# The first MLP product of eight of twelve chunks in Strassen's scheme: seven sub-products for eight, with overlaid buffers, a shared ring of PSUM banks and a new order of steps

## The chip, the cores and the metric

The kernel runs on one core of one Trainium2 chip. Times are device microseconds of that core for one execution. The kernel before takes 614.36 us (median of 3 runs, 613.46 to 614.62). Lower is better.

## The reference: what is computed

Attention over 4 batches of 8 heads, 768 positions and a head width of 64, in which a query sees its neighbours (distance under 16) and 24 block summaries. The result, laid out as 3072 rows of 512, goes through an MLP with a gelu between two products.

```python
k_sum = k.reshape(B, H, nb, block, D).max(axis=3)
v_sum = v.reshape(B, H, nb, block, D).mean(axis=3)
...
a = np.exp(scores_all)
a = a / (np.sum(a, axis=-1, keepdims=True) + 1e-09)
v_all = np.concatenate([v, v_sum], axis=2)
...
h = x @ w_in                                   # (3072, 512) @ (512, 2048)
g = 0.5 * h * (1.0 + erf(h * inv_sqrt2))
return (g @ w_out).astype(np.float32)          # (3072, 2048) @ (2048, 512)
```

## The kernel before

**Precision.** Every operand of a matmul is split into two float16 parts, hi (a cast) and lo (what the cast loses). A product is three matmuls: hi x hi, hi x lo and lo x hi. So each operand costs a cast (ScalarE, or GpSimd) and a subtraction (VectorE). The weights arrive as 64-bit floats; three bit operations on VectorE (`wi_bits`, `wo_bits`, lines 290, 295, 299) make float32 of them, `wi_hi` casts (line 306), and the lo part comes either from VectorE (line 321) or from two matmuls with an identity and a negative identity (`wi_diff`, lines 311 and 312) that ScalarE then reads (`wi_dlo`).

**Units and chunks.** The 3072 rows are 12 chunks of 256. Attention goes by 24 units: one chunk and four heads, two units to a chunk. A unit's steps: loads, `k_hi`, `q_hi`, `k_lo`, `q_lo`, `scores` (48 matmuls, line 558), `add_mask` (VectorE, line 569, reads PSUM), `maximum` over the partitions (GpSimd, line 578), `shift` (VectorE), `exponent` (ScalarE), `p_hi`, `p_lo`, `values` (52 matmuls, lines 623 and 632), a normalization of four VectorE steps (lines 643 to 657), and `x_hi`, `x_lo` (lines 671 and 675), the operand of the MLP.

**The MLP.** `phase1 c i` makes 256 of the 2048 hidden columns for chunk c: 24 matmuls of 256 columns (lines 694 to 696: two halves, four parts of the inner dimension, three products). Then `gelu` (ScalarE, line 701, from PSUM), `g_hi` (line 710) and `g_lo` (VectorE, line 714). `phase2 c i` is a quarter of the second product for half of the chunk's rows: 12 matmuls of 512 columns (lines 728 to 730), accumulated in PSUM; `store` and `put` bring the rows out. The last half chunk is cut in two columns (`phase2_cut`).

**Memory.** The eight PSUM banks are divided for good: two for the scores, two for the values, two for `phase1` (and the weight differences), two for `phase2`.

**Order.** Nothing is ordered by the compiler. `ORDER` is a list of steps written out by hand, 1315 of them; each step appends its instructions to the queues of the engines that it uses, and every engine works through its queue in that order. All DMAs are issued from one queue (SP), in the same order. A step that waits thus holds up all that stands behind it on its engine.

Of the kernel before, what the change touches and what calls it, by code (L numbers as in the profile page):

```python
# [58 lines left out]
k_lo 3, wi_hi 0, q_hi 2, p_lo 0, maximum 1, load_neg, f_mask 2, mean_vt, load_q 3, s_load_vs 0, q_lo 2, wi_diff 0 1,
fetch_w_in 6, v_hi 0, wi_diff 0 0, wi_dlo 0 1, wi_bits 1 0, scores 2, wi_dlo 0 0, wi_bits 1 1, v_diff 0 0,  # L60
s_load_vs 1, k_hi 4, fetch_w_in 5, shift 1, v_diff 0 1, v_hi 1, wi_bits 1 2, v_dlo 0 0, q_hi 3, exponent 1, warm 3,
v_diff 1 1, load_q 4, q_lo 3, v_dlo 0 1, load_v 2, p_hi 1, wi_bits 2 0, v_dlo 1 1, warm 2, values 0, wi_hi 1,
wi_bits 2 1, fetch_w_in 3, v_diff 1 0, norm_den 0, p_lo 1, evac 2, wi_diff 1 1, norm_take 0, v_dlo 1 0, f_mask 3,
maximum 2, load_mask, norm_rec 0, wi_dlo 1 1, norm_spread 0, load_k 6, scores 3, norm_mult 0, load_q 5, wi_diff 1 0,
evac 3, wi_bits 2 2, load_v 3, values 1, x_hi 0, k_hi 5, wi_dlo 1 0, x_lo 0, q_hi 4, wi_hi 2, shift 2, load_vs 2,
norm_den 1, warm 4, wi_diff 2 0, wi_bits 3 0, exponent 2, maximum 3, wi_diff 2 1, norm_take 1, load_k 7, v_hi 2,
norm_rec 1, norm_spread 1, wi_dlo 2 0, norm_mult 1, wi_dlo 2 1, warm 6, v_diff 2 0, wi_bits 3 1, x_hi 1, load_vs 3,
v_diff 2 1, v_dlo 2 0, x_lo 1, p_hi 2, v_hi 3, load_v 4, shift 3, phase1 0 0, v_dlo 2 1, q_hi 5, p_lo 2, exponent 3,
phase1 0 1, wi_bits 6 0, gelu 0 0, p_hi 3, wi_bits 6 1, load_vs 4, g_hi 0 0, p_lo 3, phase1 0 2, gelu 0 1, g_hi 0 1,
wi_bits 3 2, wi_bits 6 2, wi_hi 3, values 2, gelu 0 2, g_lo 0 0, fetch_w_in 4, wi_diff 3 0, wi_hi 6, k_lo 5,  # L70
wi_diff 3 1, g_lo 0 1, wi_dlo 3 0, g_hi 0 2, k_lo 4, wi_diff 6 0, wi_dlo 3 1, wi_bits 5 0, wi_dlo 6 0, wi_diff 6 1,
wi_bits 5 1, v_hi 4, phase1 0 3, wi_bits 5 2, wi_dlo 6 1, norm_den 2, wi_bits 4 0, fetch_w_in 7, wi_hi 5, norm_take 2,
v_diff 3 0, gelu 0 3, norm_rec 2, wi_bits 4 1, g_hi 0 3, wi_diff 5 1, v_dlo 3 0, g_lo 0 3, wi_dlo 5 1, wi_diff 5 0,
wi_bits 4 2, v_diff 3 1, wi_dlo 5 0, norm_spread 2, wi_hi 4, fetch_w_out 0, phase1 0 5, load_v 5, norm_mult 2,
v_dlo 3 1, wi_bits 7 0, x_hi 2, wi_bits 7 1, wi_diff 4 1, gelu 0 5, wi_bits 7 2, g_hi 0 5, wi_diff 4 0, wi_dlo 4 1,
g_lo 0 5, fetch_w_out 4, wi_hi 7, values 3, x_lo 2, wi_dlo 4 0, wo_bits 0 0, phase1 0 6, norm_den 3, wi_lo 7,
load_vs 5, norm_take 3, v_hi 5, norm_rec 3, phase1 0 7, norm_spread 3, gelu 0 6, norm_mult 3, g_hi 0 6, wo_bits 4 0,
x_hi 3, wo_bits 4 1, phase1 0 4, gelu 0 7, g_hi 0 7, x_lo 3, g_lo 0 6, g_lo 0 2, phase1 1 1, wo_bits 0 1, gelu 0 4,
# [5 lines left out]
fetch_w_out 6, wo_bits 5 1, wo_bits 5 2, phase2 0 1, wo_lo 3, wo_hi 5, fetch_w_out 7, q_lo 4, phase2 0 3, wo_lo 5,
load_q 6, q_lo 5, wo_bits 6 0, phase2 0 5, wo_bits 6 1, wo_bits 6 2, load_q 7, phase2 0 2, wo_bits 7 0, wo_hi 6,
fetch_k 1 0, wo_bits 7 1, wo_bits 7 2, scores 4, phase2 0 4, wo_lo 6, q_hi 6, wo_hi 7, fetch_v 1 0, k_hi 6,
add_mask 4, wo_lo 7, scores 5, maximum 4, add_mask 5, phase2 0 6, k_lo 6, g_lo 1 0, q_hi 7, load_k 8, phase2 0 7,
store 0 0, shift 4, k_hi 7, put 0 0, g_lo 1 2, exponent 4, maximum 5, v_lo 4, phase2 1 1, gelu 1 4, p_hi 4, q_lo 6,
phase2 1 3, load_v 6, store 0 1, shift 5, load_q 8, g_hi 1 4, put 0 1, p_lo 4, exponent 5, phase2 1 0, q_lo 7,
g_lo 1 4, p_hi 5, load_q 9, g_lo 1 5, phase2 1 2, prep_v 1 0, values 4, p_lo 5, phase2 1 4, norm_den 4, g_lo 1 7,  # L90
norm_take 4, gelu 1 6, norm_rec 4, norm_spread 4, phase2 1 5, norm_mult 4, g_hi 1 6, v_lo 5, x_hi 4, g_lo 1 6,
load_v 7, values 5, x_lo 4, prep_k 1 0, phase2 1 7, norm_den 5, norm_take 5, fetch_k 1 1, fetch_v 1 1, prep_k_end 1 0,
norm_rec 5, k_sums 1 0, phase2 1 6, norm_spread 5, store 1 1, norm_mult 5, put 1 1, k_lo 7, x_hi 5, x_lo 5, load_k 9,
scores 6, phase1 2 0, add_mask 6, q_hi 8, k_hi 8, prep_k 1 1, maximum 6, phase1 2 2, gelu 2 0, prep_k_end 1 1,
fetch_k 2 0, g_hi 2 0, store 1 0, prep_v 1 1, put 1 0, k_sums 1 1, phase1 2 1, gelu 2 2, g_hi 2 2, shift 6,
fetch_k 3 1, load_vs 7, phase1 2 7, gelu 2 1, g_lo 2 2, g_hi 2 1, g_lo 2 0, exponent 6, load_vs 6, q_lo 8, phase1 2 6,
k_lo 8, load_q 10, g_lo 2 1, gelu 2 7, p_hi 6, load_k 10, prep_k 3 1, scores 7, gelu 2 6, p_lo 6, v_hi 6, phase1 2 4,
q_hi 9, k_hi 9, g_hi 2 6, add_mask 7, g_hi 2 7, v_lo 6, v_hi 7, maximum 7, phase1 2 3, gelu 2 4, v_lo 7, load_v 8,
g_hi 2 4, values 6, gelu 2 3, g_hi 2 3, shift 7, phase2 2 1, norm_den 6, norm_take 6, exponent 7, load_v 9, g_lo 2 7,
load_vs 8, g_lo 2 3, phase2 2 0, k_lo 9, p_hi 7, norm_rec 6, load_k 11, norm_spread 6, p_lo 7, phase2 2 3, load_vs 9,  # L100
v_hi 8, norm_mult 6, v_lo 8, x_hi 6, values 7, x_lo 6, load_v 10, q_lo 9, phase2 2 2, norm_den 7, g_lo 2 6, load_q 11,
v_hi 9, norm_take 7, norm_rec 7, v_lo 9, scores 8, load_vs 10, norm_spread 7, phase1 2 5, q_hi 10, norm_mult 7,
k_hi 10, add_mask 8, x_hi 7, load_v 11, x_lo 7, maximum 8, scores 9, gelu 2 5, q_lo 10, phase1 3 0, g_hi 2 5,
load_vs 11, g_lo 2 5, q_hi 11, phase1 3 3, shift 8, gelu 3 0, k_hi 11, g_hi 3 0, load_q 12, g_lo 3 0, exponent 8,
q_lo 11, phase1 3 2, k_lo 10, add_mask 9, load_k 12, gelu 3 3, p_hi 8, load_q 13, g_lo 2 4, scores 10, maximum 9,
g_hi 3 3, p_lo 8, phase1 3 7, gelu 3 2, g_hi 3 2, q_hi 12, g_lo 3 2, phase1 3 5, gelu 3 7, k_hi 12, g_hi 3 7, shift 9,
g_lo 3 7, exponent 9, phase1 3 4, g_lo 3 3, k_lo 12, add_mask 10, gelu 3 5, p_hi 9, values 8, q_lo 12, maximum 10,
phase2 2 5, norm_den 8, p_lo 9, load_q 14, gelu 3 4, v_hi 10, g_hi 3 5, phase1 3 6, v_lo 10, g_hi 3 4, g_lo 3 4,
load_v 12, g_lo 3 5, phase1 3 1, gelu 3 6, norm_take 8, g_hi 3 6, shift 10, g_lo 3 6, phase2 2 7, exponent 10,
norm_rec 8, norm_spread 8, norm_mult 8, k_lo 11, gelu 3 1, p_hi 10, values 9, prep_k 2 0, load_k 13, scores 11,  # L110
g_hi 3 1, prep_k_end 2 0, v_hi 11, phase2 2 4, fetch_v 2 0, q_hi 13, g_lo 3 1, fetch_k 3 0, k_sums 2 0, q_lo 13,
x_hi 8, k_hi 13, load_k 14, v_lo 11, store 2 1, phase2 2 6, load_q 15, k_lo 13, put 2 1, load_v 13, x_lo 8,
# [749 lines left out]
```

## Time and profile before

| | |
|---|---|
| median of 3 runs | 614.36 us |
| profiled execution: span from its first to its last instruction | 612.4 us |
| TensorE (PE) busy | 604.4 us, 6050 matmuls |
| VectorE (DVE) busy | 396.4 us, 442 instructions |
| ScalarE (ACT) busy | 291.3 us, 413 instructions |
| GpSimd (POOL) busy | 162.0 us, 107 instructions |
| TensorE's granted clock | 0.999 on average |

The profile records one execution. A row of the groups gives line, engine, operation, output and inputs, count, busy time, mean nanoseconds of one, and the engine's idle time before them with what ended it. A row of the timeline gives start and duration in us. Matmuls are pipelined: the recorded duration of one (0.27 us for 256 columns) is longer than the distance to the next. The profiled execution's time beside its span is not recorded apart; its span lies 2.0 us under the median of the runs.

### The profile page before, as it was taken

The page shows a single profiled execution, that of the slowest core. Times are in us where ns is not written, and L with a number is a line of the kernel's source. Part 1 is how long each engine was busy: PE and PEld are TensorE (multiplying, and loading weights), DVE is VectorE, ACT ScalarE, POOL GpSimd, SP SyncE. Part 2 cuts the span into 40 slices and gives each one's busy share as a digit, 9 for nine tenths or more (in the row PEclk, how much of TensorE's full clock was granted, in tenths as well). Part 3 has the DMA queues.
Part 4 walks back from the last instruction along what each step waited for, and adds up shares of the span by engine and source line. Part 5 has one row for each costly group of instructions (what it writes and reads, how often), then busy time and mean ns, then how long its engine had stood idle before and what let it go on. Part 6 is the DMA issues. An engine that isn't in the chain of part 4 may idle for free.

```text
span 612.4 us, 13632 instructions
## 1 busy us (share of the span) xinstructions
PE 604.4 (99%) x6050; PEld 400.1 (65%) x6050; DVE 396.4 (65%) x442; ACT 291.3 (48%) x413; POOL 162.0 (26%) x107
## 2 busy tenths in 40 slices
...
GB/s 337 389 233 70 253 158 191 226 124 174 178 127 135 83 224 192 87 136 36 47 74 56 28 192 17 6 105 30 3 59 76 1 3 18 1 35 1 1 34 35
DMA packets 27306, 63.92 MB, mean 104 GB/s; under 512 B 2480, under 2 KB 6576, under 8 KB 26672
## 3 DMA queue, kind: packets, MB, share of 16 engines
...
HBM read 54.99 MB, written 6.29 MB: 100 GB/s over the span
## 4 chain that ended last, share of the span: by engine, by line
PE 85%; DVE 9%; DMA 2%; issue 2%; POOL 1%; ACT 1%; DVEq 0%; POOLq 0%
PE pso L728 13%; PE pso L729 13%; PE pso L730 13%; PE psh L694 12%; PE psh L695 12%; PE psh L696 12%; PE pss L558 3%; PE psv L632 2%; PE psv L623 2%; DMA kp<-in_kp_dram 1%; POOL m L578 1%; DVE wst_i L295 1%; DVE pl L594 1%; DVE ks L397 1%; PE psw_i L311 1%
## 5 line engine op out<-in xcount | busy, mean ns | idle before, releaser
L694 PE MATMUL psh<-xh,w_in_h 128*128 128x256 f16 x768 | 209.5, 273 | 0.4 <-ACT g L701 0.3
L695 PE MATMUL psh<-xl,w_in_h 128*128 128x256 f16 x768 | 209.3, 273 | 0.5 <-DVE xl L675 0.5
L696 PE MATMUL psh<-xh,w_in_l 128*128 128x256 f16 x768 | 209.3, 273 | 0.0
L728 PE MATMUL pso<-w_out_h,gh 128*128 128x512 f16 x368 | 139.7, 380 | 0.0
L729 PE MATMUL pso<-w_out_l,gh 128*128 128x512 f16 x368 | 139.5, 379 | 0.0
L730 PE MATMUL pso<-w_out_h,gl 128*128 128x512 f16 x368 | 139.5, 379 | 0.0
L714 DVE SCALAR_TENSOR_TENSOR gl<-g,gh 128x512 f16<-128x512 f32 x96 | 71.3, 758 | 90.0 <-ACT gh L710 89.8
L701 ACT ACTIVATE g<-psh 128x512 f32<-128x512 f32 x96 | 56.9, 595 | 116.3 <-PE psh L696 116.0
L578 POOL PARTITION_ALL_REDUCE m<-s x24 | 85.1, 3546 | 49.8 <-DVE s L569 37.3
L694 PEld LDWEIGHTS <-w_in_h 128*128 128x128 f16 x768 | 75.1, 98 | 12.0 <-issue 1.0
L695 PEld LDWEIGHTS <-w_in_h 128*128 128x128 f16 x768 | 75.2, 98 | 11.4 <-issue 0.9
L696 PEld LDWEIGHTS <-w_in_l 128*128 128x128 f16 x768 | 75.1, 98 | 9.3 <-issue 0.7
L710 ACT ACTIVATE gh<-g 128x512 f16<-128x512 f32 x96 | 58.9, 627 | 20.6 <-PE pso L729 18.5
L730 PEld LDWEIGHTS <-gl 128*128 128x128 f16 x368 | 36.0, 98 | 43.4
L728 PEld LDWEIGHTS <-gh 128*128 128x128 f16 x368 | 36.0, 98 | 40.2
L729 PEld LDWEIGHTS <-gh 128*128 128x128 f16 x368 | 36.1, 98 | 39.2
L590 POOL CAST ph<-s 128x1024 f16<-128x1024 f32 x24 | 31.0, 1291 | 93.1 <-PE psv L632 50.6
L532 POOL CAST qh<-q 128x512 f16<-128x512 f32 x22 | 19.8, 900 | 135.3 <-PE pss L558 135.3
L600 DVE SCALAR_TENSOR_TENSOR v_lo<-v,v_hi 128x1024 f16<-128x1024 f32 x20 | 29.3, 1470 | 22.8 <-ACT v_hi L597 22.8
L594 DVE TENSOR_TENSOR pl<-s,ph 128x1024 f16<-128x1024 f32 x24 | 34.7, 1444 | 13.0 <-POOL ph L590 13.0
L583 DVE TENSOR_TENSOR s<-s,m 128x1024 f32<-128x1024 f32 x24 | 34.7, 1444 | 11.4 <-POOL m L578 11.2
L735 ACT ACTIVATE ot<-pso 128x512 f32<-128x512 f32 x23 | 13.6, 593 | 47.6 <-PE pso L730 42.3
...
## 6 DMA issues: line engine op xcount, KB each, us to landing
...
```

The costliest lines, as they stand in the source:

```text
L578: nc.gpsimd.partition_all_reduce(out_ap=self.m32, in_ap=self.s32, channels=P, reduce_op=bass_isa.ReduceOp.max)
L583: nc.vector.tensor_tensor(out=self.s32, in0=self.s32, in1=self.m32, op=ALU.subtract)
L594: nc.vector.tensor_tensor(out=self.pl, in0=self.s32, in1=self.ph, op=ALU.subtract)
L694: nc.tensor.matmul(ph[:, e, :], w_in_h[:, k, fs], xh[:, k, :], start=(k == 0), stop=False)
L695: nc.tensor.matmul(ph[:, e, :], w_in_h[:, k, fs], xl[:, k, :], start=False, stop=False)
L696: nc.tensor.matmul(ph[:, e, :], w_in_l[:, k, fs], xh[:, k, :], start=False, stop=(k == NCC - 1))
L701: nc.scalar.activation(g32, pht.pop((c, i)), AF.Gelu, scale=1.0 / (SC_X * SC_WI))
L710: nc.scalar.activation(gh, g32t[c, i], AF.Copy, scale=SC_G)
L714: nc.vector.scalar_tensor_tensor(out=gl, in0=g32t.pop((c, i)), scalar=SC_G, in1=gh, op0=ALU.mult, op1=ALU.subtract)
L728: nc.tensor.matmul(p, gh[:, f, js], w_out_h[:, f, :], start=(f == 0), stop=False)
L729: nc.tensor.matmul(p, gh[:, f, js], w_out_l[:, f, :], start=False, stop=False)
L730: nc.tensor.matmul(p, gl[:, f, js], w_out_h[:, f, :], start=False, stop=(f == NFC - 1))
```

## The change

The chunks 4 to 11 are taken by pairs (4 and 5, 6 and 7, and so on). For a pair, x is a matrix of two by two blocks: A11 and A12 the even chunk's two halves of the inner dimension, A21 and A22 the odd chunk's; `w_in` has B11, B12, B21, B22 by halves of the inner dimension and of the hidden columns. Four blocks of the result take eight block products as they stand. Strassen's scheme, in Winograd's form, takes seven:

- S1 = A21 + A22, S2 = S1 - A11, S3 = A11 - A21, S4 = A12 - S2 (`sx_add`, on VectorE, for every pair); T1 = B12 - B11, T2 = B22 - T1, T3 = B22 - B12, T4 = B21 - T2 (`t_add`, once);
- P1 = A11 B11, P2 = A12 B21, P3 = S4 B22, P4 = A22 T4, P5 = S1 T1, P6 = S2 T2, P7 = S3 T3, each a `product` of 12 matmuls for a column group j (256 columns of each half; j from 0 to 3);
- the results are P1 + P2 (even chunk, first half), P1 + P6 + P5 + P3 (even, second), P1 + P6 + P7 + P4 (odd, first) and P1 + P6 + P7 + P5 (odd, second).

P1, P6, P7 and P4 are accumulated one after the other in one PSUM bank; between them `keep` (ScalarE) copies the state to SBUF three times, and `h_add` (VectorE) adds a copy to another bank, for three of the four results. `gelu` then works in place. The sums S and T get hi and lo parts of their own: seven x casts and subtractions for a pair instead of four, and eight `t_hi` and `t_lo`.

The float32 words of `w_in` are kept (`w32`) until the T are made, and the parts of T are written over them. To make room, tiles share memory: the staging tile later holds x parts and sums, `k32` first holds `w_out` words, the identity lies in the mask's tile and the output tile in the 16-bit mask's, hsum lies over the part of `w_in` that only chunks 0 to 3 use, and `p_h`, `p_l` and the x parts have one copy or fixed places. The scores and the values keep two PSUM banks each; all else takes the next free bank of a ring of four. In batch 0 and around, many casts go from GpSimd to ScalarE (`s_k_hi` 14 times for 2, `s_q_hi` 12 for 2, `s_p_hi` 16 for 0, `s_load_vs` 5 for 2). The order, now 1536 steps, is written anew from the first step to the last.

```diff
+PAIRS = (2, 3, 4, 5)
+class Ring:
+    def use(self, key, uses):
+        if key not in self.held:
+            self.held[key] = [self.free.pop(0), 0]
+        tenant = self.held[key]
+        tenant[1] += 1
+        if tenant[1] == uses:
+            self.free.append(self.held.pop(key)[0])
+        return tenant[0]
...
-fetch_k 0 0, load_m16, load_q 0, fetch_k 0 1, fetch_vt 0, prep_k 0 0, s_k_hi 0, load_ind, warm 20, f_mask 0,
+load_q 0, fetch_k 0 0, k_hi 0, s_q_hi 0, q_lo 0, prep_k 0 0, k_lo 0, prep_k_end 0 0, k_sums 0 0, fetch_w_in 0,
...
+load_v 1, fetch_w_in 1, evac 0, s_k_hi 1, load_neg, wi_hi 0 0, wi_hi 0 1, warm 1 4, f_mask 1, wi_diff 0 0, wi_dlo 0 0,
+prep_k_end 0 1, wi_diff 0 1, k_sums 0 1, k_lo 1, warm 2 1, scores 1, s_k_hi 2, s_q_hi 2, maximum 0, shift 0, q_lo 2,
+wi_bits 2 0, k_lo 2, wi_dlo 0 1, evac 1, exponent 0, maximum 1, s_p_hi 0, s_k_hi 3, sum_vt 0, sum_vt 1, sum_vt 2,
+mean_vt, f_mask 2, scores 2, shift 1, p_lo 0, wi_bits 2 1, wi_bits 1 0, wi_bits 2 2, wi_bits 1 1, k_lo 3, wi_bits 1 2,
...
+sx_lo 2 1, norm_mult 10, t_lo 0 0, p_lo 11, shift 12, k_lo 13, phase2 3 3, phase2 3 6, values 11, product 2 0 1,
+product 2 0 2, phase2 3 5, t_lo 0 1, norm_den 11, load_v 12, norm_take 11, norm_rec 11, norm_spread 11, norm_mult 11,
...
+product 2 0 7, sx_add 2 6, p_sx_hi 2 6, keep 2 0 2, t_add 3 2, h_add 2 1 0, t_add 2 3, sx_lo 2 6, k_lo 14,
...
+    ps_s = ps.tile([P, UCOLS], F32, name="ps_s")
+    ps_v = ps.tile([P, UCOLS], F32, name="ps_v")
+    bank = Ring("bank", [ps.tile([P, 512], F32, name=f"bank{i}") for i in range(4)])
...
+    hsum = [late[:, i * 1024 : (i + 1) * 1024].bitcast(F32) for i in range(3)]
+    w32 = [const.tile([P, 2, WP], F32, name=f"w32_{i}") for i in range(4)]
...
+    wst_ring = Ring("wst", [k32[:, :WP]])
...
+    def t_add(i, n):
+        b11, b21, b12, b22 = (w32[i][:, f, k * 512 : (k + 1) * 512] for f in range(2) for k in range(2))
+        out, in0, in1, op = (
+            (b22, b22, b12, ALU.subtract), (b12, b12, b11, ALU.subtract),
+            (b11, b22, b11, ALU.add), (b21, b21, b11, ALU.subtract),
+        )[n]
+        nc.vector.tensor_tensor(out=out, in0=in0, in1=in1, op=op)
+    def t_hi(i, e):
+        dst = t_hl[i][0].rearrange("p t k f -> p (t k f)")[:, e * WP : (e + 1) * WP]
+        nc.scalar.activation(dst, w32[i][:, e], AF.Copy, scale=SC_WI)
+    def t_lo(i, e):
+        h, l = (a.rearrange("p t k f -> p (t k f)")[:, e * WP : (e + 1) * WP] for a in t_hl[i])
+        nc.vector.scalar_tensor_tensor(out=l, in0=w32[i][:, e], scalar=SC_WI, in1=h, op0=ALU.mult, op1=ALU.subtract)
...
+    PRODUCTS = {
+        1: (SX, A11, (0, 0), True), 6: (SX, S2, T2, False), 7: (SX, S3, T3, False), 4: (SX, A22, T4, False),
+        2: (SY, A12, (1, 0), True), 5: (SZ, S1, T1, True), 3: (SZ, S4, (1, 1), False),
+    }
+    USES = {SX: 8, SY: 2, SZ: 4}
+    def acc(p, j, a):
+        return bank.use(f"s{p}_{j}{a}", USES[a])
+    def product(p, j, m):
+        a, xi, w, first = PRODUCTS[m]
+        t = acc(p, j, a)
+        xh, xl = x_hl[xi]
+        for e in range(2):
+            dst = t[:, e * CH : (e + 1) * CH]
+            for k in range(KH):
...
+                for n, (l, r) in enumerate(((wh, xh), (wh, xl), (wl, xh))):
+                    nc.tensor.matmul(
+                        dst, l, r[:, k], start=(first and e == 0 and k == 0 and n == 0),
+                        stop=(k == KH - 1 and n == 2), skip_group_check=True,
+                    )
+    def keep(p, j, n):
+        nc.scalar.activation(hsum[n], acc(p, j, SX), AF.Copy)
+    def h_add(p, j, n):
+        c, i = 2 * p + n // 2, j + 4 * (n % 2)
+        g = g_ring.use(f"{c}_{i}", 4)
+        a, s = ((SY, 0), (SZ, 1), None, (SZ, 2))[n]
+        nc.vector.tensor_tensor(out=g, in0=acc(p, j, a), in1=hsum[s], op=ALU.add)
...
-    nc = _bacc.Bacc("TRN2", target_bir_lowering=False, num_devices=1)
+    nc = _bacc.Bacc("TRN2", target_bir_lowering=False, num_devices=1, dynamic_dma_scratch_size=512)
```

More of the change, by code (lines that the diff above doesn't have):

```diff
@@ L59 @@
[L59 to L78, printed above, removed]
@@ L84 @@
[L84 to L103, printed above, removed]
@@ L104 @@
[L104 to L112, printed above, removed]
-prep_v 2 0, phase2 3 1, norm_den 9, prep_k 3 0, fetch_k 2 1, phase2 3 3, load_k 15, add_mask 11, fetch_v 2 1,
@@ new lines @@
+phase2 1 7, add_mask 6, norm_take 5, norm_rec 5, norm_spread 5, norm_mult 5, load_k 8, fetch_v 3 0, s_q_hi 8,
+s_k_hi 8, maximum 6, q_lo 8, load_vs 6, put 0 1, x_hi 5, store 1 0, x_lo 5, q_lo 7, shift 6, phase1 2 2, phase1 2 0,
+v_hi 6, t_add 1 0, t_add 2 0, v_lo 6, k_lo 8, put 1 0, load_vs 7, load_k 9, fetch_k 2 0, load_q 10, load_k 10,
+exponent 6, v_hi 7, store 1 1, v_lo 7, load_v 9, load_q 9, scores 7, phase1 2 1, add_mask 7, scores 8, s_p_hi 6,
+q_hi 10, s_k_hi 9, p_lo 6, values 6, phase1 2 4, prep_k 2 0, add_mask 8, gelu 2 0, k_lo 9, gelu 2 2, gelu 2 1,
@@ new lines @@
+norm_rec 7, norm_spread 7, g_lo 2 4, prep_k_end 2 1, g_lo 2 5, norm_mult 7, g_hi 2 6, x_hi 7, scores 9, load_k 12,
+put 1 1, load_q 12, fetch_v 2 0, t_add 1 1, x_lo 7, add_mask 9, prep_v 3 0, t_add 3 0, load_k 11, phase1 3 6,
+phase1 3 2, exponent 8, g_hi 2 7, s_p_hi 8, maximum 9, k_hi 11, g_lo 2 6, prep_v 2 0, scores 10, gelu 3 6, p_lo 8,
+add_mask 10, shift 9, gelu 3 2, phase1 3 0, phase1 3 5, values 8, fetch_v 3 1, load_q 11, load_v 10, fetch_k 3 1,
+prep_v 3 1, g_lo 2 7, k_lo 11, t_add 1 2, prep_k 3 1, gelu 3 5, norm_den 8, norm_take 8, norm_rec 8, gelu 3 0,
@@ new lines @@
+prep_v 2 1, q_lo 12, g_lo 3 3, norm_den 9, norm_take 9, shift 11, phase2 2 5, phase2 3 0, phase2 2 7, t_add 2 1,
+g_hi 3 4, v_hi 11, t_add 2 2, prep_k_end 3 0, store 2 0, norm_rec 9, g_lo 3 4, sx_hi 2 0, v_hi 10, norm_spread 9,
+sx_lo 2 0, v_lo 11, exponent 11, g_lo 3 5, t_hi 0 1, g_hi 3 7, g_lo 3 7, p_lo 10, phase2 3 2, scores 12, phase2 3 4,
+v_lo 10, t_add 0 3, norm_mult 9, values 10, p_sx_hi 2 1, norm_den 10, add_mask 12, put 2 0, store 2 1, t_hi 0 0,
+norm_take 10, norm_rec 10, norm_spread 10, phase2 3 1, load_k 13, s_k_hi 13, s_p_hi 11, k_hi 14, maximum 12,
@@ new lines @@
+load_k 17, k_hi 17, add_mask 15, load_vs 15, load_q 17, maximum 15, s_q_hi 17, k_lo 16, load_k 18, p_hi 14, gelu 5 6,
+h_add 2 3 1, gelu 4 7, p_sx_hi 3 0, g_hi 5 6, v_hi 15, norm_den 13, g_hi 4 7, product 2 3 4, phase2 4 5, phase2 5 1,
+g_lo 5 2, k_lo 17, shift 15, v_lo 14, g_lo 4 7, phase2 4 6, scores 16, p_lo 14, sx_lo 3 0, norm_take 13, phase2 4 7,
+norm_rec 13, norm_spread 13, g_hi 5 7, q_lo 17, v_lo 15, norm_mult 13, values 14, add_mask 16, load_v 16, put 3 1,
+k_sums 3 0, gelu 5 3, store 4 0, norm_den 14, g_hi 5 3, exponent 15, prep_k_end 3 1, norm_take 14, norm_rec 14,
```

651 lines of the change are left out of this document (368 added, 283 removed).

## The prediction

> **What bounds the kernel now.** The page of the profile comes first: its span and its busy times.
>
> ```profile
> span 612.4 us, 13632 instructions
> PE 604.4 (99%) x6050; PEld 400.1 (65%) x6050; DVE 396.4 (65%) x442; ACT 291.3 (48%) x413; POOL 162.0 (26%) x107
> ```
>
> TensorE is busy 99% of the span, but a busy share does not say whether the work is needed or dense. So I read the span in three stages, cut where the first product begins (46.26) and where chunk 4 begins (236.33).
>
> ```profile
> core 0: us, PE busy (x) PEld busy (x) DVE busy (x) ACT busy (x) POOL busy (x), PEclk, DMA share, GB/s
> 0.00:46.26 46.26, 43.18 (x413) 19.20 (x414) 40.22 (x40) 29.40 (x41) 29.73 (x26) 1.00 0.85 317
> 46.26:236.33 190.07, 188.22 (x1986) 126.83 (x1986) 179.17 (x189) 110.33 (x150) 61.29 (x38) 1.00 0.52 164
> 236.33:612.40 376.07, 373.04 (x3658) 254.03 (x3652) 176.99 (x214) 151.55 (x222) 70.96 (x44) 1.00 0.16 48
> ```
>
> The clock is at 1.00 throughout. In the last stage VectorE (DVE) works 177 of 376 us: TensorE alone sets the time. In the middle one DVE works 179 of 190: it is nearly as late as TensorE. Then the density, in order of time (start, duration):
>
> ```profile
> 480.32 0.27 PE L694 MATMUL psh<-xh,w_in_h 128*128 128x256 f16 x1
> ...
> 482.94 0.27 PE L694 MATMUL psh<-xh,w_in_h 128*128 128x256 f16 x1
> ```
>
> ```profile
> 536.30 0.38 PE L728 MATMUL pso<-w_out_h,gh 128*128 128x512 f16 x1
> ...
> 538.89 0.38 PE L728 MATMUL pso<-w_out_h,gh 128*128 128x512 f16 x1
> ```
>
> Between the first pair of rows lie 24 matmuls (one `phase1`): 2.62/24 = 0.109 us each, back to back. Between the second lie 12 (one `phase2`): 2.59 us. A matmul taken out of this stream is worth its 0.109.
>
> **The change part by part. Removed.** For each pair of chunks and each of four column groups j, eight sub-products of 12 matmuls become seven: 16 x 12 = 192 matmuls fewer, of the same 256 columns. 192 x 0.109 = **20.9 us** off TensorE. Start-up matmuls (`warm`) fall from 52 to 40, but these fill waits and give nothing by themselves.
>
> **Start-up.** What ends last before the first product is DVE's `x_lo 1`:
>
> ```profile
> 5.37 1.75 DVE L397 TENSOR_REDUCE ks<-w_out_l 128x48 f32<-128x1536 f32 x1 [5.37 <-DMA w_out_l<-in_kp_first_dram]
> ...
> 10.57 0.81 DVE L539 TENSOR_TENSOR k_lo<-w_out_l,k_hi 128x640 f16<-128x640 f32 x1
> ```
>
> ```profile
> 12.16 2.51 DVE L539 TENSOR_TENSOR k_lo<-w_out_l,k_hi 128x640 f16<-128x640 f32 x1
> ```
>
> ```profile
> 12.05 3.27 POOL L578 PARTITION_ALL_REDUCE m<-s  x1
> ```
>
> ```profile
> 46.10 1.52 DVE L675 TENSOR_TENSOR xl<-den,xh 128x512 f16<-128x512 f32 x1
> ```
>
> ```profile
> 73.18 0.69 DVE L714 SCALAR_TENSOR_TENSOR gl<-g,gh 128x512 f16<-128x512 f32 x1 [0.43 <-ACT gh L710]
> 73.79 0.68 DVE L675 TENSOR_TENSOR xl<-den,xh 128x512 f16<-128x512 f32 x1
> ```
>
> The same `k_lo` takes 0.81 us alone and 2.51 beside a GpSimd maximum (+1.69, rounded apart); `x_lo` takes 0.68 alone and 1.52 beside a GpSimd cast. From the 2.51 row to the 46.10 row, and one cast just before, 13 DVE instructions are stretched so, 9.7 us in all. With 5.4 us of waiting for the first load that leaves 47.6 - 15.1 = 32.5 us of DVE work up to the end of `x_lo 1`. The new order asks for three more bit steps (two of L290, one of L299):
>
> ```profile
> 60.58 0.70 DVE L290 TENSOR_SCALAR wst_i<-wraw_i 128x1024 int32<-128x1024 int32 x1
> 61.31 1.23 DVE L295 SCALAR_TENSOR_TENSOR wst_i<-wraw_i,wst_i 128x1024 int32<-128x1024 int32 x1
> 62.57 1.23 DVE L299 SCALAR_TENSOR_TENSOR wst_i<-wraw_i,wst_i 128x1024 int32<-128x1024 int32 x1
> ```
>
> 2 x 0.73 + 1.2 = 2.7, so 35.2. GpSimd loses most of its casts to ScalarE (ACT) here: six instructions, three of them maxima, instead of sixteen with four. I take a little over half of the stretch: 5.2. The first load now stands behind `load_q 0`: 6 instead of 5.4. A new wait: `shift 1` stands on DVE only 2.1 us of work behind `shift 0`, while `maximum 1` must first see two `wi_diff`, `scores 1`, `evac 1`; I estimate 3 us (0 to 4; 3.3 is one whole maximum), and all DVE work behind it is late by that. `x_lo 1` then ends at 35.2 + 6 + 5.2 + 3 = 49.4, and the first product starts, as now, 1.4 before: 48. Ahead of it stand two more `wi_diff` and two more `v_diff`, each
>
> ```profile
> 61.08 1.02 PE L311 MATMUL psw_i<-wst_i,eye 128*128 128x512 f32 x2
> 61.94 0.38 PE L312 MATMUL psw_i<-w_in_h,neg 128*128 128x512 f16 x1
> 62.15 0.27 PE L694 MATMUL psh<-xh,w_in_h 128*128 128x256 f16 x1
> ```
>
> 1.07 us, which later stages need no more: 46.26 + 4.3 = 50.5 would be no change, so start-up gains **2.5**. Bounds: a gain of 8 (neither stretch nor wait) and a loss of 5 (ACT, busy 29.4 us now and given the casts, some 8 us, becomes the late one).
>
> **Middle stage,** first product to the first Strassen product. It gains two `phase2`, one `values` and one `scores`:
>
> ```profile
> 117.19 0.81 PE pss L558 x48
> ...
> 137.15 0.55 PE psv L623 x4
> 137.70 0.76 PE psv L632 x48
> ```
>
> 5.2 + 1.3 + 0.8 less the 4.3 moved out: 190.07 + 3.0 = 193.1 if TensorE sets it. DVE gets 13 of the 16 `t_add`, three more `prep_v`, and a unit's steps earlier. Prices: `t_add`, `sx_add`, `sx_lo` and `h_add` by L675 above, whose neighbour starts 0.6 apart; the rest from
>
> ```profile
> L600 DVE SCALAR_TENSOR_TENSOR v_lo<-v,v_hi 128x1024 f16<-128x1024 f32 x20 | 29.3, 1470 | 22.8 <-ACT v_hi L597 22.8
> L735 ACT ACTIVATE ot<-pso 128x512 f32<-128x512 f32 x23 | 13.6, 593 | 47.6 <-PE pso L730 42.3 <-DMA out_dram<-ot 5.2
> ```
>
> ```profile
> L450 DVE TENSOR_REDUCE vs<-vb 96x64 f32<-96x2048 f32 x6 | 13.6, 2275 | 1.3 <-DMA vb<-in_vb_dram 1.3
> ```
>
> (`prep_v` 2.3 by L450; `t_lo` by L600's form, 1.47 at most as its mean holds stretched ones, and nearer the 1.23 of L299). DVE's 179.2 holds 17.8 of stretch, in 20 instructions from the 46.10 row to
>
> ```profile
> 220.16 1.17 DVE L545 TENSOR_TENSOR ql<-q,qh 128x512 f16<-128x512 f32 x1 [0.93 <-POOL qh L532]
> ```
>
> so 161.4 net. Added are 7.8 (`t_add`) and 6.9 (`prep_v`), and 5 for the rest: `add_mask`, two `shift`, `p_lo`, a normalization (2.4, below), two `prep_k_end`, two `sx_lo`, a `t_lo` are 10, and two `x_lo`, a `q_lo` and three bit steps go, 5. Together 181. What stretch comes on top? A normalization beside a maximum is not stretched:
>
> ```profile
> 34.82 0.70 DVE L643 STREAM_TRANSPOSE dent<-den 128x512 f32<-128x512 f32 x1
> ...
> 36.67 0.69 DVE L657 TENSOR_TENSOR den<-psv,dent 128x512 f32<-128x512 f32 x1
> ```
>
> ```profile
> 34.22 3.77 POOL L578 PARTITION_ALL_REDUCE m<-s  x1 [2.86 <-ACT s L565]
> ```
>
> In the new order a reduction or a normalization step stands first or second after `add_mask` 4 to 12, where the maximum starts (all but 8); the old order has a `v_lo`, `p_lo` or `q_lo` in that place, 1.69 longer, for six of these nine. I take 4 us of stretch (0 to 17.8): DVE needs 185 of 193. All `kp` and `vb` loads now come in this stage, since their tile holds x later; L450's row shows 1.3 us of waiting for them, and I add none. DVE begins about 1 us late, so I charge **+1.5** (0 to +10: 181 + 17.8 = 199, some waits, against 193.1).
>
> **Last stage.** TensorE needs what it needs now less 20.9 and the steps moved forward (7.3). New beside it: 48 `keep` on ACT (L735's form, 0.593: 28.5 us), 48 `h_add` (28.8), 16 `sx_add`, 12 more `sx_lo`, the last `t_lo` on DVE: at most 177.0 + 28.8 + 9.6 + 7.2 + 8.5 + 1.8 = 233 us, while ACT has 151.6 + 28.5 + 8.5 (`t_hi`) + 7.6 (`sx_hi`) + 9 (casts) = 205, both in 348: covered. What can show is the handover. Products 1, 6, 7, 4 share one bank; each must wait until `keep` has copied the state before. The latency:
>
> ```profile
> 609.15 0.22 PE L746 MATMUL pso<-w_out_h,gl 128*128 128x128 f16 x1
> ```
>
> ```profile
> 609.41 0.28 ACT L749 ACTIVATE ot<-pso 128x128 f32<-128x128 f32 x1 [2.14 <-PE pso L746]
> ```
>
> 0.04 from matmul end to ACT; a 256-column matmul drains 0.27 - 0.11 = 0.16 after its slot; so 0.16 + 0.04 + 0.59 + 0.04 (the way back, taken as equal) = 0.83, where the order leaves one other product, 12 x 0.109 = 1.31, in 16 of 64 handovers and 2 us or more in the others. The shared ring adds nine bank changes with one product between. Only where ACT or DVE is inside another operation (0.6 to 1.06 us) is it missed, by 0.1 to 0.6, so over 25 places **+2** (0 to +10). There is one output tile as before; some `put` now stand on SP behind loads that wait for their buffer, the next `store` waits on ACT for the landing, and `gelu` behind it. The L735 row puts such waits at 5.2 us in all now, hidden by TensorE's other work; I add none (bound 3). `k32` now holds `w_out` words until `wo_lo 7`: `load_k 6` is late, but five `phase2` and a `values` (14 us) lie before `scores 6`. The tail is the same.
>
> **Sum.** 612.4 - 20.9 - 2.5 + 1.5 + 2 = 592.5. The median of the runs, 614.36, lies 2.0 above the span: **594.5**.
>
> **Rivals.** *ACT falls behind the handovers.* Slower than before if all 64 lose over 0.34 us each (2 + 19.9 to make up): ACT would have to run 2 us behind TensorE in all 16 groups. At 0.45 each: 594.5 - 2 + 28.8 = 621. For: `keep` stands between `gelu` and `g_hi` in the queue. Against: ACT's work is 205 of 348. 5%.
>
> *DVE is stretched in the middle as before.* All added DVE steps but `h_add` read two operands in SBUF, as the stretched ones do. Nine maxima x 1.69 = 15.2 plus casts: the stage takes 10 more, 594.5 + 8.5 = 603. Against: the order above. 17%. [...] The trace bears out who is hit but not for how long: the 2.51 us `k_lo` ended 0.65 before its maximum did; 1% of the 17 is for it.
>
> *ACT bounds start-up:* first product at 55 instead of 48, 601.5. For: 8 us more work on ACT, much of it in chains. 12%.
>
> *No new stalls:* 594.5 - 3.5 - 3 = 588. 10%. That the products do not shrink can be excluded by counting; that some load now binds and eats all: 2%, no change.
>
> **Numbers.** Forecast (590 to 599) 54%. Range 588 to 604, which leaves out the first rival and part of the last. A difference under 0.2% (1.2 us) can't be told from none. Faster 0.93, same 0.02, slower 0.05.
>
> **What would show it.** Right: 192 fewer matmuls of 256 columns at the same spacing of 0.109; first product near 48; DVE over 90% busy until the first Strassen product at about 243; gaps in front of products 6, 7, 4, 3 summing to some 2 us. Wrong if those gaps exceed 10 us, if DVE instructions beside maxima are again 1.69 longer, or if the first product comes after 52.

## The result and the profile after

The changed kernel takes 590.7 us (median of 4 runs, 589.77 to 591.95) against 614.24 for the kernel before: 0.9618 of its time, 95% interval 0.9601 to 0.9635. The prediction said 594.5, in a range of 588 to 604. The profiled execution is the slowest of the four (591.95 us, span 590.2); the spans of the other three are 588.3, 588.0 and 588.9. First the page's head, then the same three stages as before, cut at the first product (50.50) and at the first Strassen product (240.84).

```profile
span 590.2 us, 13402 instructions
...
PE 582.6 (99%) x5846; PEld 381.7 (65%) x5846; DVE 429.4 (73%) x543; ACT 342.4 (58%) x515; POOL 120.5 (20%) x77
```

```profile
core 0: us, PE busy (x) PEld busy (x) DVE busy (x) ACT busy (x) POOL busy (x), PEclk, DMA share, GB/s
0.00:50.50 50.50, 47.29 (x412) 21.14 (x413) 37.09 (x43) 35.42 (x54) 17.17 (x18) 0.97 0.80 290
50.50:240.84 190.34, 190.22 (x2099) 129.31 (x2098) 181.23 (x217) 118.62 (x173) 35.76 (x16) 1.00 0.53 169
240.84:590.20 349.36, 345.07 (x3342) 231.26 (x3336) 211.11 (x284) 188.34 (x289) 67.60 (x43) 1.00 0.16 49
```

TensorE has 204 matmuls fewer: 192 of the products and 12 `warm`. VectorE (DVE) and ScalarE (ACT) carry 33 and 51 us more, and TensorE is still busy 99% of the span. By stages: the start-up is 4.2 us longer (and does 4.3 us of weight differences that stood later before), the middle stage is as long as it was though it holds 3.0 us more of TensorE's work, the last stage is 26.7 us shorter.

The mean clock of the start-up is 0.97. In steps of 1 us (TensorE's busy time, then the granted clock) the changed kernel's profile has

```profile
34.00:35.00 1.00, 0.48 (x2) 1.00 1.06 414
35.00:36.00 1.00, 0.00 (x0) 1.00 1.02 356
36.00:37.00 1.00, 0.84 (x2) 1.00 0.93 336
37.00:38.00 1.00, 0.82 (x3) 0.83 0.93 311
38.00:39.00 1.00, 1.00 (x2) 0.50 0.93 350
...
40.00:41.00 1.00, 1.00 (x7) 0.50 1.01 377
41.00:42.00 1.00, 1.00 (x51) 0.96 1.11 393
```

Behind a wait of 1.7 us (34.5 to 36.2) TensorE ran at half its clock for 3.4 us (37.7 to 41.1), which costs up to 1.7. Not every execution has this. The experiment product_2_twice below has the same start-up and middle stage, at full clock:

```profile
0.00:48.78 48.78, 45.57 (x412) 20.74 (x413) 36.99 (x43) 35.31 (x54) 17.57 (x18) 1.00 0.84 300
48.78:238.90 190.12, 190.12 (x2100) 129.33 (x2098) 181.64 (x217) 118.51 (x173) 35.76 (x16) 1.00 0.53 169
238.90:608.10 369.20, 365.71 (x3533) 250.05 (x3528) 209.78 (x284) 189.03 (x289) 68.38 (x43) 1.00 0.15 46
```

So the first product comes at 48.8, and with the last stage of 349.4 from the changed kernel's profile the span is 238.9 + 349.4 = 588.3, where the other executions are.

The very start differs between executions too. The order opens with 33 `warm` matmuls. Here they are in the changed kernel's profile, then in that of wait_filled (below), which has the same order up to 32 us:

```profile
0.97 10.24 PE L778 MATMUL bank<-ones 128*64 128x512 f16 x33 [0.97 <-POOL ones L349]
```

```profile
0.97 8.62 PE L778 MATMUL bank<-ones 128*64 128x512 f16 x33 [0.97 <-POOL ones L349]
```

In the first 14 of them follow one another at 0.427 us, in the second 6; nearly all others at 0.216. In the changed kernel's profile this block is the head of the chain of waits. `evac 2` on ScalarE (L654) starts at 27.01 in the one and 25.23 in the other, but from there to the first product it is 21.8 us (without the 1.7 of the half clock) and 21.9. So first products of two profiles that lie less than 2 us apart say little about an edit, and three of the start-up experiments are read from `evac 2` on, which stands ahead of their edits.

### The profile page after: what moved, and what is told of

Its sections match the earlier page's. It is cut to its first block, busy times and chain, and to the rows that moved or that the text cites. A ratio compares the mean times of both kernels' runs of the same rounds, so it can differ in the third digit from the quotient of the medians.

```text
span 590.2 us, 13402 instructions
## 1 busy us (share of the span) xinstructions
PE 582.6 (99%) x5846; PEld 381.7 (65%) x5846; DVE 429.4 (73%) x543; ACT 342.4 (58%) x515; POOL 120.5 (20%) x77
## 3 DMA queue, kind: packets, MB, share of 16 engines
q1 hardware_dynamic: 27248, 63.06, 32.6%
## 4 chain that ended last, share of the span: by engine, by line
PE 81%; DVE 9%; ACT 4%; DMA 3%; issue 2%; POOL 1%; SPq 0%; DVEq 0%; ACTq 0%; POOLq 0%
PE bank L816 24%; PE bank L864 11%; PE bank L865 11%; PE bank L866 11%; PE bank L789 4%; PE bank L790 4%; PE bank L791 4%; PE ps_v L718 3%; PE ps_s L648 2%; PE bank L424 2%; PE ps_v L709 2%; PE bank L778 2%; DMA stage<-in_vb_dram 1%; DVE p_l L682 1%; DMA stage<-in_w_out_dram 1%
## 5 line engine op out<-in xcount | busy, mean ns | idle before, releaser
L864 PE MATMUL bank<-w_out_h,gh 128*128 128x512 f16 x368 | 139.6, 379 | 0.0
L865 PE MATMUL bank<-w_out_l,gh 128*128 128x512 f16 x368 | 139.5, 379 | 0.0
L866 PE MATMUL bank<-w_out_h,gl 128*128 128x512 f16 x368 | 139.5, 379 | 0.0
L816 PEld LDWEIGHTS <-w 128*128 128x128 f16 x640 | 62.3, 98 | 8.8
L816 PEld LDWEIGHTS <-w_in 128*128 128x128 f16 x576 | 55.9, 98 | 9.8
L828 DVE TENSOR_TENSOR g<-bank,late 128x512 f32<-128x512 f32 x48 | 32.9, 685 | 35.5 <-PE bank L816 25.3
L789 PE MATMUL bank<-x,w_in 128*128 128x256 f16 x192 | 52.4, 273 | 0.0
L790 PE MATMUL bank<-x,w_in 128*128 128x256 f16 x192 | 52.3, 273 | 0.0
L791 PE MATMUL bank<-x,w_in 128*128 128x256 f16 x192 | 52.3, 273 | 0.0
L822 ACT ACTIVATE late<-bank 128x512 f32<-128x512 f32 x48 | 28.1, 590 | 36.2 <-PE bank L816 27.9
L816 PE MATMUL bank<-x,w_in 128*128 128x256 f16 x384 | 46.2, 273 | 0.0
L816 PE MATMUL bank<-x,w 128*128 128x256 f16 x320 | 43.5, 273 | 0.0
L816 PE MATMUL bank<-stage,w 128*128 128x256 f16 x320 | 43.5, 273 | 0.0
L837 ACT ACTIVATE g<-g 128x512 f32<-128x512 f32 x48 | 29.6, 625 | 19.9 <-DVE g L828 19.8
```

The lines of the kernel that those rows point to most:

```text
L789: nc.tensor.matmul(dst, wh, xh, start=(k == 0), stop=False)
L790: nc.tensor.matmul(dst, wh, xl, start=False, stop=False)
L791: nc.tensor.matmul(dst, wl, xh, start=False, stop=(k == NCC - 1))
L816: nc.tensor.matmul(dst, l, r[:, k], start=(first and e == 0 and k == 0 and n == 0), stop=(k == KH - 1 and n == 2), skip_group_check=True,)
L828: nc.vector.tensor_tensor(out=g, in0=acc(p, j, a), in1=hsum[s], op=ALU.add)
L837: nc.scalar.activation(g, h, AF.Gelu, scale=1.0 / (SC_X * SC_WI))
```

## The experiments

Each stands beside runs of the kernel before on the same chip. The changed kernel's 590.7 is the measure for the differences; first products and stages are read from each run's profile.

| run | median us (range) | of the time before (95%) |
|---|---|---|
| product_2_twice | 610.56 (609.39 to 613.77) | 0.9943 (0.9925 to 0.9961) |
| eight_plain | 618.35 (616.97 to 621.01) | 1.0071 (1.0049 to 1.0092) |
| eight_plain_2 | 618.8 (616.6 to 620.59) | 1.0061 (1.0041 to 1.008) |
| keep_twice | 599.22 (598.92 to 602.02) | 0.9768 (0.9738 to 0.9797) |
| beside_maxima | 607.47 (606.56 to 608.24) | 0.988 (0.9861 to 0.9899) |
| ahead_of_masks | 597.26 (595.73 to 598.23) | 0.9712 (0.9688 to 0.9737) |
| start_scalar_more | 595.74 (594.84 to 597.44) | 0.9693 (0.9671 to 0.9716) |
| start_vector_more | 594.67 (593.99 to 594.81) | 0.967 (0.965 to 0.969) |
| start_two_to_gpsimd | 590.28 (589.36 to 591.56) | 0.9609 (0.9589 to 0.963) |
| start_prep_k_later | 588.54 (587.75 to 588.8) | 0.9574 (0.9559 to 0.9589) |
| start_evac_later | 588.3 (587.78 to 590.21) | 0.9575 (0.9557 to 0.9593) |
| wait_filled | 589.75 (588.35 to 592.77) | 0.9602 (0.9577 to 0.9627) |

**What a product is worth: product_2_twice.**

```diff
-        for e in range(2):
+        for e in (0, 1, 0, 1) if m == 2 else (0, 1):
```

> Product 2 of every group is computed twice into the same bank, 12 matmuls more in each of 16 groups; everything else is as in the changed kernel. Theory (each product lies on TensorE's path at its full 12 x 0.109): 590.7 + 20.9 = 611.6, within 1 us. Rival (TensorE waits for the other engines somewhere in the last stage, so that the extra work fills the wait): 605 or less, and the gaps in front of the products gone.

19.9 us more. The last stage grew from 349.36 to 369.20, by 19.84; a product twice over is 16 x 1.31 = 21.0. The 1.1 between them is in the gaps: the start-to-start times of the products exceed 12 (or 24) x 0.109 by 2.2 us in all in the changed kernel's profile and by 1.0 here. What TensorE waited for by name in the last stage, in the changed kernel and here (waits by line: total, times, longest):

```profile
PE bank L816 <- ACT late L822: 0.8, 1, 0.8
PE ps_v L709 <- DVE p_l L682: 0.5, 1, 0.5
```

```profile
PE ps_v L709 <- DVE p_l L682: 0.5, 1, 0.5
```

A product lies on TensorE's path with its whole length. The rival (waits that extra work would fill) has 1 us, not 6.

**Eight plain products in the new order: eight_plain and eight_plain_2.**

```diff
-        1: (SX, A11, (0, 0), True), 6: (SX, S2, T2, False), 7: (SX, S3, T3, False), 4: (SX, A22, T4, False),
-        2: (SY, A12, (1, 0), True), 5: (SZ, S1, T1, True), 3: (SZ, S4, (1, 1), False),
+        1: (0, 0, [(A11, (0, 0))]), 2: (0, 0, [(A12, (1, 0))]),
+        6: (1, 4, [(A21, (0, 1))]), 5: (1, 4, [(A22, (1, 1))]),
+        7: (1, 0, [(A21, (0, 0))]), 4: (1, 0, [(A22, (1, 0))]),
+        3: (0, 4, [(A11, (0, 1)), (A12, (1, 1))]),
```

> The order, the buffers and the bank ring of the changed kernel, but eight plain products for each pair of chunks and column group: the sums S and T, their casts, the keeps and the h_adds are left out, gelu reads the bank where h_add stood, and five products stand a few places later because a bank is held longer. Theory (TensorE alone is late, and the side work of Strassen's scheme is hidden but for the 2.4 us of gaps in front of products): 590.7 + 192 x 0.109 - 2.4 = 609, up to 612 if the moved products wait. Rival (the scheme's own work on VectorE and ScalarE costs 5 us or more, given back elsewhere): 606 or less. Rival (the new order is what makes the kernel faster, the scheme little): 595 to 600.

> Eight plain products again, this time with the even chunk's second half in the places of products 6 and 5 and the odd chunk's second half in that of product 3, so that no operand is overwritten before its use: it computes the reference. Theory (the scheme is worth its 20.9 us less the 2 us of gaps that it makes): 588.7 + 20.9 and what the longer held banks cost (6.7 us of waits in front of products in eight_plain, less here if the wrong operands made some of them): 610 to 617. Rival (the new order is worth much by itself): under 606.

The edit shown is that of eight_plain; eight_plain_2 has A11 and A12 in the places of products 6 and 5, A21 and A22 in that of product 3. In both, some late column groups of the second and third pair of chunks (pairs 3 and 4 in the order) multiply the next pair's A11 and A12, whose casts the order has already put into the same place; so neither computes quite the reference, the second against its expectation. By their medians both are slower than all expectations (the second by 1.8 us). These are TensorE's waits in the last stage of eight_plain:

```profile
PE bank L806 <- ACT g L823: 2.7, 4, 0.7
PE bank L850 <- ACT g L823: 2.2, 1, 2.2
PE ps_v L691 <- DVE p_l L664: 0.9, 2, 0.5
PE bank L806 <- ACT mask_sb L855: 0.7, 1, 0.7
```

The first two lines, 4.9 us, are banks that a plain result holds until `gelu` has read it; the other 1.6 are waits for `p_l` and for `store`. The profiled span is 615.4 at full clock; the first product comes at 48.4, the middle stage takes 190.6, and the last stage 376.4 against 349.4. Without these 6.5 us 608.9 would be left, 20.6 above 588.3: what eight products cost, with nothing given back by the side work that is left out. That subtraction is an argument, not a measurement; what the new order alone would be worth with well placed banks stays open.

**The handover's reserve: keep_twice.**

```diff
-        nc.scalar.activation(hsum[n], acc(p, j, SX), AF.Copy)
+        t = acc(p, j, SX)
+        for _ in range(2):
+            nc.scalar.activation(hsum[n], t, AF.Copy)
```

> Each of the 48 keeps copies the bank twice in a row, so that a handover takes 0.83 + 0.5 = 1.3 to 1.4 us where it took 0.83. Theory (a handover has 1.31 us, one product, in 16 places and 2.6 or more in the others): 0.1 us lost in each of the 16, and some more where ScalarE is late, 592 to 594. Rival (ScalarE stands right behind the handovers with no reserve): 48 x 0.5 = 24 us more, 610 or more.

8.5 us more, between the theory's 3 and the rival's 20. Its last stage, and what TensorE waited for in it:

```profile
238.78:597.10 358.32, 347.89 (x3341) 231.50 (x3336) 210.45 (x284) 215.96 (x337) 68.80 (x43) 1.00 0.15 48
```

```profile
PE bank L816 <- ACT late L824: 4.7, 9, 1.2
PE bank L866 <- ACT g L839: 1.2, 2, 1.0
PE bank L816 <- DVE g L830: 0.8, 2, 0.6
PE ps_v L709 <- DVE p_l L682: 0.5, 1, 0.5
```

The stage is 9.0 us longer than the changed kernel's, and the product gaps rise from 2.2 to 7.8 us. Nine waits for a `keep` of 0.5 on average and up to 1.2, not sixteen of 0.1: a `keep` is late where ScalarE has other work queued ahead of it, and the second copy makes the whole queue longer. The changed kernel has one such place, in front of a product 7 (TensorE's row, then ScalarE's):

```profile
254.86 0.38 PE L816 MATMUL bank<-stage 128*128 128x256 f16 x2 [0.81 <-ACT late L822]
```

```profile
253.27 1.06 ACT L447 ACTIVATE w<-w 128x1024 f16<-128x1024 f32 x1 [1.07 <-DVE w L451]
254.23 0.58 ACT L822 ACTIVATE late<-bank 128x512 f32<-128x512 f32 x1
```

The `keep` (L822) stood behind `t_hi` (L447), and that had waited 1.07 us for VectorE.

**VectorE beside a maximum: beside_maxima and ahead_of_masks.** The step `extra` is two subtractions of 512 elements; in the first run it stands behind, in the second ahead of `add_mask`.

```diff
-wo_hi 5, add_mask 4, maximum 4, wo_lo 5, prep_k 1 0, ...
+wo_hi 5, add_mask 4, extra, maximum 4, wo_lo 5, prep_k 1 0, ...
```

> Two more VectorE subtractions of 512 elements with both inputs in SBUF (results unused, 0.6 us each) right behind each add_mask of units 4 to 12, where the GpSimd maximum starts: 18 x 0.6 = 10.8 us more VectorE work. If an operation in this place is stretched by 1.69 as before: up to 9 x 1.69 = 15 us on top, VectorE needs 181 + 26 = 207 of the middle stage's 190, the total is 602 to 608. If there is no stretch: as in the control, 591 to 595. If the operation is shut out for the whole maximum (3.3 us each): 9 x 3.3 = 30 us on top, 615 or more.

> The control: the same 18 subtractions, but ahead of each add_mask of units 4 to 12, where no maximum runs: 10.8 us more VectorE work, unstretched. The middle stage has 190.3 us, and VectorE is busy 181.2 of it, so 192 is asked: 591 to 595. If VectorE's reserve in this stage is really none, because each wait is already placed to the last: up to 601.

10.2 us lie between the two. The pair in unit 5, beside the maximum and in the control, and the maximum:

```profile
130.87 2.98 DVE L891 TENSOR_TENSOR dent<-mask_sb 128x512 f16<-128x512 f32 x2
```

```profile
131.14 3.49 POOL L665 PARTITION_ALL_REDUCE m<-s  x1 [16.49 <-ACT gh L847]
```

```profile
128.97 1.41 DVE L891 TENSOR_TENSOR dent<-mask_sb 128x512 f16<-128x512 f32 x2
```

2.98 against 1.41. In six of the nine places the second of the pair, which starts 0.4 to 0.6 us after the maximum, lasts 2.26 instead of 0.68: 6 x 1.58 = 9.5 us. In the other three the maximum comes 2.7 us or more after the pair's start, and the pair keeps its time. In the control two of the 18 are longer, by 0.9 us in all (one of them ran into a maximum after all). The middle stage takes 206.8 us (the expectation asked 207) and the control 196.7; VectorE is busy 8.2 us longer than there. TensorE's waits of 3.8 and 3.0 us that follow are followed in turn by two more phases of 3.4 us at half clock (the mean clock is 0.992), which at up to 1.7 us each can make up the rest of the 10.2; that is argued, not measured. In the changed kernel's middle stage the nearest to such an instruction is a `k_lo` 0.9 us after a maximum, which is 0.83 longer. The control itself is 6.6 us slower for 10.8 us of added work, above its 591 to 595: VectorE is idle 9 us of this stage, but in these places only about 4 of them took up work.

**Who bounds the start-up: start_scalar_more, start_vector_more, start_two_to_gpsimd.**

```diff
-s_load_vs 0, v_hi 0, load_vs 1, v_diff 0 1, v_diff 0 0, evac 2, v_hi 1, ...
+s_load_vs 0, v_hi 0, load_vs 1, v_diff 0 1, v_diff 0 0, evac 2, v_hi 1, v_hi 1, v_hi 1, v_hi 1, ...
```

> In the start-up ScalarE does one cast (v_hi of unit 1) four times in a row, 3 x 0.95 = 2.9 us more work ahead of 30 us. Theory (ScalarE bounds the start-up): the first product comes 2.9 us later, total 593.6. Rival (VectorE bounds it): ScalarE has room, total 590.7 to 591.5.

> In the start-up VectorE does one subtraction (k_lo of unit 3) five times in a row, 4 x 0.74 = 3.0 us more work ahead of 31 us. Theory (ScalarE bounds the start-up, VectorE has room behind 37 us): total 590.7 to 591.7. Rival (VectorE bounds it): first product 3 us later, total 593.7.

The changed kernel's chain of waits shows why ScalarE was suspected; from 27.9 to 37.6 there is nothing else in it:

```profile
24.94 1.99 DVE p_l L682
...
27.93 1.05 ACT v_hi L685
28.98 0.97 ACT v_lo L703 x2
29.95 0.95 ACT s L673
30.90 1.03 ACT w_in L381 x2
31.94 0.58 ACT den L724
...
32.54 1.06 ACT v L597
...
37.14 0.50 ACT v_lo L703
37.64 0.04 issue
37.68 2.08 PE bank L424 x2
```

From 37.7 to the first product TensorE itself is busy without a named wait. With 4.31 - 1.05 = 3.3 us more on ScalarE the first product comes at 53.4, 26.5 after `evac 2` (26.87) instead of 21.9: 4.6 more. A half-clock phase of 3.4 us is in that, at most 1.7 of loss, so 2.9 or more of the 3.3 come through. On VectorE the five `k_lo` took more than was meant (6.11 for five, 0.81 for one: 5.3 added), by the author's estimate since they ran into a maximum (at 33.40 for 3.21 us in the changed kernel's profile):

```profile
30.17 6.11 DVE L632 TENSOR_TENSOR k_lo<-w_out_l,k_hi 128x640 f16<-128x640 f32 x5
36.20 1.22 DVE L375 SCALAR_TENSOR_TENSOR w<-gl,w 128x1024 int32<-128x1024 int32 x1
```

The first product comes at 53.1, 26.8 after `evac 2` (26.34), 4.9 more than 21.9, with 6.8 us on end at half clock (38.3 to 45.2, at most 3.4 of loss) in it. So 1.5 to 4.9 of the 5.3 come through, and the total alone, 4.0 us, would not have told the two engines apart. VectorE has a reserve of 0.4 to 3.8 us here, ScalarE at most 0.4.

```diff
-s_load_vs 2, q_hi 3, s_p_hi 1, v_hi 2, ...
+load_vs 2, q_hi 3, p_hi 1, v_hi 2, ...
```

> Two ScalarE steps of the start-up go back to GpSimd: the copy of the means for unit 2 (load_vs) and the cast p_hi of unit 1, 2.1 us of ScalarE work ahead of 37.7 us. Theory (ScalarE bounds the start-up from 27 to 37.7 us): first product 2 us earlier, at 48.5, total 588.7 to 589.5. Rival (VectorE bounds it, as the prediction had it): first product unchanged, 590.7, or later by the stretch that the two GpSimd casts put on VectorE, 591.5.

The first product comes at 48.0, 20.8 after `evac 2` (27.22): 1.1 of the 2.1 us moved are gained. (In the next experiment, with the same two casts moved, it is 21.6, so 0.2 to 1.1.) The total doesn't gain what was expected. In the profiled execution, the slowest of the four (span 589.8, the others 587.6 to 588.1), the middle stage is 2.3 us longer, 192.63. There VectorE waits for a load that was 0.83 late in the changed kernel:

```profile
165.85 1.75 DVE L495 TENSOR_REDUCE ks<-stage 128x48 f32<-128x1536 f32 x1 [0.83 <-DMA stage<-in_kp_dram]
```

```profile
165.64 1.75 DVE L495 TENSOR_REDUCE ks<-stage 128x48 f32<-128x1536 f32 x1 [3.10 <-DMA stage<-in_kp_dram]
```

This is `prep_k 2 1`; `norm_mult 6` and `p_lo 7` stand behind it on VectorE, and `values 7` on TensorE waits for these. The earlier start is only a part of it: this load, issued at 159.46, took 6.2 us until VectorE could start, in the changed kernel (161.18) 4.7. keep_twice and wait_filled have first products at 48.6 and 47.1 and wait 0.62 and 1.15 us for it, 4.6 us after its issue. So about 1.5 of the 3.10 are a slow load in this one execution; why it was slow stays open.

**The load taken off the path: start_prep_k_later, and one more wait: start_evac_later.**

```diff
-norm_spread 6, prep_k 2 1, t_add 0 0, norm_mult 6, g_lo 2 0, p_lo 7, t_add 0 1, ...
+norm_spread 6, t_add 0 0, norm_mult 6, g_lo 2 0, p_lo 7, prep_k 2 1, t_add 0 1, ...
```

> As start_two_to_gpsimd, and in addition VectorE's reduction prep_k 2 1, which there waited 3.1 us for its load at 162.5 us, stands behind p_lo 7 instead of ahead of norm_mult 6. Theory (the two casts gave 0.6 to 1.1 us at the start, and this load, issued by SP behind load_vs 9, took it back: VectorE waits, values 7 waits for VectorE): first product at 48.0, the 1.5 us in front of values 7 and the 1.2 in front of it gone, total 590.3 - 2.5 = 587.8 (587.3 to 588.5). Rival (VectorE is simply out of time in the middle stage): values 7 waits as before, 590.

> As start_prep_k_later, and in addition ScalarE's evac 2, which waits 1.1 us for VectorE's p_lo 0 with v_hi 1 queued behind it, stands behind v_hi 1. Theory (ScalarE's queue bounds the start-up, so that each microsecond that it does not stand still is one gained): first product at 47.0, the 1.0 us in front of v_diff 1 1 gone, total 586.8. Rival (VectorE is next, with a reserve of some 2.6 us in the start-up but less in the middle): the first product comes earlier, the middle stage gives it back, 587.8 or more.

The first gives the middle stage back its 190.04 us and TensorE no named wait in it; `p_lo 7` starts at 163.78 instead of 169.11:

```profile
161.00 0.71 DVE L734 STREAM_TRANSPOSE dent<-rec 128x512 f32<-128x512 f32 x1
...
163.78 1.73 DVE L682 TENSOR_TENSOR p_l<-s,p_h 128x1024 f16<-128x1024 f32 x1
165.44 1.74 DVE L495 TENSOR_REDUCE ks<-stage 128x48 f32<-128x1536 f32 x1
```

At 588.54 us this version beats both kernels: 0.9574 of the time before, and its interval (to 0.9589) lies below that of the changed kernel (from 0.9601). How much of this is the load and how much the earlier start isn't told apart: its profile's first product, at 47.2, is of an execution with a short opening (`evac 2` at 25.55). The second edit, expected to give 1 us more, gives no difference that can be told: its first product comes at 46.9 against 47.2, and the wait of 1.0 us in front of `v_diff 1 1` was not there in start_prep_k_later either.

**The half clock: wait_filled.**

```diff
-v_dlo 1 1, warm 3 2, v_diff 2 0, ...
+v_dlo 1 1, warm 3 11, v_diff 2 0, ...
```

> The changed kernel with 11 warm matmuls in place of 2 where TensorE waits 2.3 us at 34 to 36 us (warm 3). They take 9 x 0.213 = 1.9 us of the wait. Theory (TensorE's clock is halved for some 3.3 us after a wait of 2 us or more, in some executions): the clock stays at 1.0 in every execution, first product at 48.6, total 589.8 to 590.7, and no execution 2 us above the others. Rival (the halving has another cause): some executions still show it. If the wait is no real wait: later by up to 1.9 us.

589.75 us, about the 590.7 of the changed kernel; in its profiled execution the wait is filled (TensorE is busy 5.00 of the 5 us from 33 to 38) and the clock at 1.00 throughout. But one of its five executions has a mean clock of 0.997 and takes 592.77. Where the half clock lies in that one isn't recorded. The theory that this wait alone brings the half clock falls; what decides whether an execution has it stays open.

## Why the prediction was right, and where its steps were not

- **Products, -20.9.** Right. The last stage came out at 349.4 where the prediction's terms give 376.1 - 20.9 - 7.3 + 2 = 349.9, and the products cost 19.8 us when put back, with 1.1 of gaps filled.
- **Handovers, +2.** Right in size, partly by luck: the products' start-to-start times exceed their work by 2.2 us, but not as 25 misses of 0.1; the one named wait for a handover is 0.81. The reason holds in part. A handover of 0.83 in a gap of 1.31 doesn't show; one that is 0.5 longer costs 9 us of the 24, 6.7 of it in thirteen named waits for ScalarE or VectorE. The rival "ACT falls behind the handovers" has one place in the changed kernel, for 0.81 us.
- **Start-up, first product at 48.** 48.8 at full clock, 50.5 in the profiled execution: near, but that it came near is luck, for the step "what ends last before the first product is DVE's x_lo 1" failed. `shift 1` waited 0.56 for `maximum 1`, not 3, and the stretch was 2.9 us in three instructions, not 5.2. ScalarE, with the casts it was given, took the place: the rival's engine, at a price far under its 55. That `warm` matmuls "fill waits and give nothing by themselves" doesn't hold for the first 33: they stand at the head of the chain with 10.24 us in the changed kernel's profile, and 8.6 to 10.2 from execution to execution. The half clock was no term at all.
- **Middle stage, +1.5 on 193.1.** Wrong by 4.3 us: 190.3, and 190.1 at full clock. The step that failed is "190.07 + 3.0 = 193.1 if TensorE sets it": it took the old stage as dense. There TensorE was busy 188.22 of 190.07, and 1.5 us of its waits were named:

```profile
PE psv L623 <- DVE den L657: 0.5, 1, 0.5
PE psh L695 <- DVE xl L675: 0.5, 1, 0.5
PE psh L694 <- ACT g L701: 0.3, 1, 0.3
PE psw_i L311 <- DVE wst_i L299: 0.2, 1, 0.2
```

  Each step's start-to-start time less the median of its kind sums to 4.7 us in the old stage and to 2.0 in the new one. These 2.7 and the 1.5 that was charged and not paid are the 4.3.
- **VectorE in the middle.** Right in the mechanism: 181.2 us busy (185 were asked), 3.5 of them stretch (4 taken), none of 1.69. The rival "DVE is stretched in the middle as before" was real as a price: put behind `add_mask`, the same kind of instruction costs 1.58 each and the stage 10 us. The 1% of the 17 is for a price well above 1.69: no run shows one, and the longest stretch of one instruction in the profiles of the two kernels is 1.7 us. Nor is every VectorE instruction beside a maximum stretched: in the changed kernel a `q_lo` with two SBUF inputs started 2.2 us into a maximum and took its usual 0.68:

```profile
147.39 0.68 DVE L637 TENSOR_TENSOR ql<-q,qh 128x512 f16<-128x512 f32 x1
```

```profile
145.22 3.22 POOL L665 PARTITION_ALL_REDUCE m<-s  x1 [11.98 <-ACT k_lo L508]
```

- **Loads in the middle, "I add none".** Right for this kernel by a narrow margin: one load was 0.83 us late, and in start_two_to_gpsimd, where the start-up was faster and the load itself 1.5 slower, it was 3.10 late and cost 2.3.
- **Sum.** 592.5 for the span against 590.2 in the profile and 588.0 to 588.9 in the other executions: the miss is the middle stage's 4.3, with the start-up 0.8 the other way at full clock.
